# Attention with an MLP in float32 pieces: forms of the early units, g written over h, and new due times

## Chip, cores and metric

The kernel runs on one core of a Trainium2 chip. The metric is the device time of one execution in microseconds; three runs of the kernel before gave a median of 235.07 us (234.83 to 237.4).

## What is computed

A linear attention with a quadratic feature map, 4 batches, 4 heads, 1088 positions, head size 32, and behind it an MLP on 4352 tokens of 128 features with 2048 hidden units. All in float32; the inputs arrive as float64 words for the weights and for S, which the kernel turns into float32 itself.

```python
def phi(x):
    a = np.einsum('rd,bhsd->bhsr', S1, x)
    b = np.einsum('rd,bhsd->bhsr', S2, x)
    return np.einsum('bhsi,bhsj->bhsij', a, b).reshape(*x.shape[:-1], r * r)
kv = np.einsum('bhsf,bhsd->bhfd', k_p, v)
num = np.einsum('bhsf,bhfd->bhsd', q_p, kv)
den = np.einsum('bhsf,bhf->bhs', q_p, z)[..., None] + 1e-06
h = x @ w_in
g = np.where(h >= 1, h, np.where(h <= -1, 0.0, (h + 1) ** 2 / 4))
out = g @ w_out
```

## The kernel before

**Attention.** For each batch b, `keys(b, ...)` projects the keys with S (tiles abk, then transposed to kab), forms the products kp, sums z over them and builds kv and its turned copy kvb. `queries(b, ...)` does the same for the queries (abq, cq for the denominator, den, ap, qp, the transposed qt) and gathers the result into nd, from which x_hi and x_lo are cut: x rounded to float32r, and the rest. Batch 0 is done in four groups of positions, numbered 0 to 3 (nd0_1 is the gather of group 1), batches 1 to 3 in one gather of four banks each (nd1 is that of batch 1).

**The MLP.** The tokens lie in 9 chunks of 512 (the last has 256). A unit u is one chunk with one block j of 128 hidden units; there are 144. The first two chunks are woven in runs of four units, and so are the last two; the others follow each other. `unit(u)` (line 799) does the following:

- TensorE: h, three passes of float32r (x_hi wi_hi, x_lo wi_hi, x_hi wi_lo; L807 to L809) into one PSUM bank.
- ScalarE: s from h (L822), and its square (L824).
- VectorE: the clamp of h and s to g (L827).
- In most units g is split into g_hi, rounded to float32r, and g_lo, the rest (L838). TensorE adds three passes to the chunk's accumulator acc (L848, L849, L852).
- In a direct unit the clamp alone is made, and TensorE multiplies g as it stands with the whole piece of w_out (o32) in float32, L855; such a product shows as two passes in the trace.

So a unit has one of four kinds, for which this document uses the letters of the change:

| kind | g lies in | g_hi by | g_lo by | down product |
|---|---|---|---|---|
| w | SBUF | none | none | one in float32 |
| v | SBUF | VectorE, a second clamp | GpSimd | three passes |
| c | SBUF | ScalarE, a cast (L834) | GpSimd | three passes |
| p | PSUM | ScalarE, a cast | VectorE | three passes |

Before, the kind follows from shares by stretch: FP (w), IN_PSUM (p) and HI_ACT (c). A p unit holds two banks, that of h and one more for g.

**The weights.** `weights` loads pieces of 512 columns (i0 to i3, o0 to o3) into three raw buffers; `from_double` (line 395) makes the float32 value in several steps on ScalarE, GpSimd and VectorE, with a bank m (mi, mo) in between, and cuts it into hi (ScalarE) and lo (GpSimd). Where units of a group of four blocks are w, the piece of w_out is kept whole in o32.

**The order.** The program is written out by a planner, class Plan (line 91). Each step has a due time, an engine, an estimated cost, what it reads and what it writes. The planner plays the engines forward, and each free engine takes the ready step that is due first and has its buffers. There are 8 PSUM banks in the ring ps. The resulting order is fixed: on the chip each engine takes its instructions one after the other and waits at a semaphore where an input is not there. Due times come from tables: FK, FKV and FQ (keys and queries of batch 0), KEYS, QEND and QLONG (the later batches, counted in units), LOADS (their loads), I0, I1, WI, O0, O1, WO and OW (the weights). KP_POOL and QP_POOL name the pieces of kp and qp that GpSimd makes; the others are VectorE's. Until 15.82 us of its own time the planner fills TensorE's pauses with products of ones, called warm.

```python
plan.add(u, "PE", 3 * rounded(n), up, r=[...], w=[h]).kind(0, 6)
g = bank(f"g{u}") if late else Buf("g_hi", f"gd{u}", [P, CH]) if direct else Buf("g", f"g{u}", [P, CH])
plan.add(u, "DVE", dve(n), lambda: clamp(g), r=[h, s], w=[g])
if tag == "o" and c in fp_units:
    keep = whole[c] = Buf("o32", f"o32_{c}", [P, WC])
```

## Time and profile before

| what | value |
|---|---|
| median of three runs | 235.07 us (234.83 to 237.4) |
| span of the profiled execution, first to last instruction | 233.1 us |
| TensorE (PE) busy | 225.6 us, 97% |
| VectorE (DVE) busy | 197.9 us, 85% |
| ScalarE (ACT) busy | 191.8 us, 82% |
| GpSimd (POOL) busy | 195.1 us, 84% |
| DMA, mean over the span | 59 GB/s |

The profiled execution is described by its span; what lies around it is the difference to the time of a run. Busy times are unions of an engine's instructions; instructions of one engine overlap by some 0.1 us, so from one start to the next it takes less than one lasts. PEld are the weight loads of TensorE, which lie beside its passes. In a timeline a bracket at the end of a row tells the idle time of the engine before it and what ended it, as inferred from semaphores.

### The profile page before, as it was taken

The page shows a single profiled execution, that of the slowest core. Times are in us where ns is not written, and L with a number is a line of the kernel's source. Part 1 is how long each engine was busy: PE and PEld are TensorE (multiplying, and loading weights), DVE is VectorE, ACT ScalarE, POOL GpSimd, SP SyncE. Part 2 cuts the span into 40 slices and gives each one's busy share as a digit, 9 for nine tenths or more (in the row PEclk, how much of TensorE's full clock was granted, in tenths as well). Part 3 has the DMA queues.
Part 4 walks back from the last instruction along what each step waited for, and adds up shares of the span by engine and source line. Part 5 has one row for each costly group of instructions (what it writes and reads, how often), then busy time and mean ns, then how long its engine had stood idle before and what let it go on. Part 6 is the DMA issues. An engine that isn't in the chain of part 4 may idle for free.

```text
span 233.1 us, 4932 instructions
## 1 busy us (share of the span) xinstructions
PE 225.6 (97%) x1741; PEld 171.1 (73%) x1743; DVE 197.9 (85%) x379; ACT 191.8 (82%) x388; POOL 195.1 (84%) x175
## 2 busy tenths in 40 slices
PE   7979999999999999999999999999999999999994
PEld 2646656767768867876788688888788888888893
DVE  2479999999776989998869999997999589679983
ACT  3257999999998997884799669997897899499994
POOL 5796608678676799999998999999979899969991
PEclk9999999999999999999999999999999999999999
DMA  6960770750001100001000010001000100010001
...
DMA packets 4775, 13.86 MB, mean 59 GB/s; under 512 B 528, under 2 KB 912, under 8 KB 4752
## 3 DMA queue, kind: packets, MB, share of 16 engines
...
q8 instruction: 13, 0.21, 0.4%
q14 instruction: 10, 0.08, 0.1%
...
## 4 chain that ended last, share of the span: by engine, by line
PE 90%; DMA 4%; DVE 2%; issue 1%; ACT 1%; POOL 0%; SPq 0%; POOLq 0%
PE h L807 13%; PE acc L852 13%; PE h L808 13%; PE h L809 13%; PE acc L848 12%; PE acc L849 12%; PE acc L855 5%; DMA q<-in_qT 2%; PE nd L748 2%; DMA k<-in_kT 2%; PE kv L564 2%; PE warm L334 1%; PE abq L611 1%; PE abk L505 1%; PE cq L617 1%
## 5 line engine op out<-in xcount | busy, mean ns | idle before, releaser
L838 POOL TENSOR_TENSOR g_lo<-g,g_hi 128x512 fp32r<-128x512 f32 (+1 forms) x121 | 146.9, 1246 | 14.3 <-DVE g_hi L827 9.0
L827 DVE SCALAR_TENSOR_TENSOR g<-h,s 128x512 f32<-128x512 f32 (+1 forms) x131 | 83.7, 649 | 18.6 <-ACT s L824 15.6
L822 ACT ACTIVATE s<-h 128x512 f32<-128x512 f32 (+1 forms) x144 | 79.6, 572 | 16.0 <-PE h L809 13.3
L824 ACT ACTIVATE s<-s 128x512 f32<-128x512 f32 (+1 forms) x144 | 85.1, 613 | 2.2
L827 DVE SCALAR_TENSOR_TENSOR g_hi<-h,s 128x512 fp32r<-128x512 f32 (+1 forms) x98 | 63.9, 656 | 1.7 <-POOL g_lo L838 0.9
L807 PE MATMUL h<-x_hi,wi_hi 128*128 128x512 f32 (+1 forms) x144 | 58.0, 403 | 0.1
L808 PE MATMUL h<-x_lo,wi_hi 128*128 128x512 f32 (+1 forms) x144 | 54.9, 381 | 0.0
L809 PE MATMUL h<-x_hi,wi_lo 128*128 128x512 f32 (+1 forms) x144 | 54.6, 379 | 0.0
L848 PE MATMUL acc<-g_hi,wo_hi 128*128 128x512 f32 (+1 forms) x131 | 50.6, 388 | 0.0
L849 PE MATMUL acc<-g_hi,wo_lo 128*128 128x512 f32 (+1 forms) x131 | 49.4, 377 | 0.0
L852 PE MATMUL acc<-g_lo,wo_hi 128*128 128x512 f32 (+1 forms) x131 | 46.6, 389 | 0.0
L807 PEld LDWEIGHTS h<-x_hi,wi_hi 128*128 128x128 f32 x144 | 27.1, 188 | 8.1 <-PE h L809 0.6
L808 PEld LDWEIGHTS h<-x_lo,wi_hi 128*128 128x128 f32 x144 | 27.1, 188 | 6.5 <-issue 1.7
L809 PEld LDWEIGHTS h<-x_hi,wi_lo 128*128 128x128 f32 x144 | 27.1, 188 | 5.3
L852 PEld LDWEIGHTS acc<-g_lo,wo_hi 128*128 128x128 f32 x131 | 24.3, 188 | 7.0 <-issue 2.1
L848 PEld LDWEIGHTS acc<-g_hi,wo_hi 128*128 128x128 f32 x131 | 24.6, 188 | 6.2 <-issue 1.4
L849 PEld LDWEIGHTS acc<-g_hi,wo_lo 128*128 128x128 f32 x131 | 24.6, 188 | 4.7 <-issue 0.5
L834 ACT CAST g_hi<-g 128x512 fp32r<-128x512 f32 (+1 forms) x33 | 18.2, 562 | 2.6 <-DVE g L827 2.4
L529 POOL TENSOR_TENSOR kp<-kab 128x768 f32<-128x768 f32 (+2 forms) x8 | 15.1, 1901 | 2.9 <-DVE kab L511 2.9
L649 POOL TENSOR_TENSOR qp<-ap,qab 128x768 f32<-128x768 f32 x8 | 12.0, 1516 | 1.5 <-DVE ap L644 1.5
L855 PE MATMUL acc<-gd,o 128*128 128x512 f32 x26 | 12.9, 592 | 0.0
L827 DVE SCALAR_TENSOR_TENSOR gd<-h,s 128x512 f32<-128x512 f32 x13 | 8.7, 679 | 0.8 <-ACT s L824 0.8
(100 smaller groups left out, 176.7 us busy)
## 6 DMA issues: line engine op xcount, KB each, us to landing
...
```

The source lines that it names most:

```text
L807: nc.tensor.matmul(t[:, :n], lhsT=wi_hi[:, fj], rhs=x_hi[:, xs], start=True, stop=False)
L808: nc.tensor.matmul(t[:, :n], lhsT=wi_hi[:, fj], rhs=x_lo[:, xs], start=False, stop=False)
L809: nc.tensor.matmul(t[:, :n], lhsT=wi_lo[:, fj], rhs=x_hi[:, xs], start=False, stop=True)
L822: plan.add(u, "ACT", act(n), lambda: nc.scalar.activation(of(s)[:, :n], of(h)[:, :n], AF.Relu, bias=0.5, scale=0.5), r=[h], w=[s])
L824: plan.add(u, "ACT", act(n, False), lambda: nc.scalar.activation(of(s)[:, :n], of(s)[:, :n], AF.Square), w=[s])
L827: nc.vector.scalar_tensor_tensor(out=of(out)[:, :n], in0=of(h)[:, :n], scalar=1.0, in1=of(s)[:, :n], op0=ALU.max, op1=ALU.min)
L834: plan.add(u, "ACT", act(n, False), lambda: nc.scalar.copy(of(g_hi)[:, :n], of(g)[:, :n]), r=[g], w=[g_hi])
L838: plan.add(u, "DVE" if late else "POOL", dve(n) if late else pool_t(n), lambda: eng.tensor_tensor(out=of(g_lo)[:, :n], in0=of(g)[:, :n], i ...
L848: nc.tensor.matmul(of(acc)[:, :n], lhsT=wo_hi[:, fj], rhs=of(g_hi)[:, :n], start=first, stop=False)
L849: nc.tensor.matmul(of(acc)[:, :n], lhsT=wo_lo[:, fj], rhs=of(g_hi)[:, :n], start=False, stop=False)
L852: nc.tensor.matmul(of(acc)[:, :n], lhsT=wo_hi[:, fj], rhs=of(g_lo)[:, :n], start=False, stop=last)
L855: nc.tensor.matmul(of(acc)[:, :n], lhsT=of(whole[j // JW])[:, j % JW * P : (j % JW + 1) * P], rhs=of(g)[:, :n], start=first, stop=last)
```

## The change

Four things change.

1. The kinds of units 0 to 47 are spelled out in a word, KINDS; later units are c by a share CAST = 0.23 and v otherwise; the last four are p as before. FP, IN_PSUM and HI_ACT are gone.
2. A p unit has no bank of its own for g: the clamp writes over h.
3. `from_double` may leave a weight piece's value in its bank m and split it there, for the pieces named in IN_BANK = ('o0',), unless the piece is kept whole.
4. Nearly all due times and both lists of GpSimd's pieces have new numbers. KP_POOL gains (1, 0), QP_POOL loses (3, 0) and (3, 2).

Counted from the two rules, units of each kind:

| units | before | after |
|---|---|---|
| 0 to 31 | w 13, v 9, c 6, p 4 | w 8, v 8, c 11, p 5 |
| 32 to 47 | v 11, c 3, p 2 | v 8, c 5, p 3 |
| 48 to 143 | v 78, c 14, p 4 | v 71, c 21, p 4 |

```diff
-FP = (0.86, 0.57, 0.27, 0)
-OW = (2.26, 14.08, 3.92, 10.35)
+KINDS = 'wwwcpwwcwvcwvpcvvwcpvccccpvvpccvvvvvcvvvccppcvcp'
+IN_BANK = ('o0',)
+CAST = 0.23
+OW = (1.48, 6.15, 3.08, -14.76)
...
-LOADS = {1: (-1.49, 7.13, -0.36), 2: (9.25, 9.39, 31.26), 3: (58.3, 55.18, 44.56)}
-HI_ACT = (0.86, 0.38, 0.22, 0.15)
+LOADS = {1: (-1.2, 3.71, -5.47), 2: (17.53, 13.45, 26.52), 3: (55.55, 68.14, 43.66)}
...
-        full = keep or mag
+        banked = not keep and tag in IN_BANK
+        full = mb if banked else keep or mag
...
-                out=of(full).bitcast(I32), in0=lw(), scalar=29, in1=m(),
+                out=m() if banked else of(full).bitcast(I32), in0=lw(), scalar=29, in1=m(),
...
-        plan.add(due, "ACT", act(n, False), lambda: nc.scalar.copy(hi, of(full)), r=[full], w=[toks[0]])
-        plan.add(due, "POOL", pool_t(n), lambda: nc.gpsimd.tensor_tensor(
-            out=lo, in0=of(full), in1=hi.bitcast(F32), op=ALU.subtract), r=[full, toks[0]], w=[toks[1]])
+        value = lambda: of(full)[:, :n]
+        plan.add(due, "ACT", act(n, banked), lambda: nc.scalar.copy(hi, value()), r=[full], w=[toks[0]])
+        eng = nc.vector if banked else nc.gpsimd
+        plan.add(due, "DVE" if banked else "POOL", dve(n) if banked else pool_t(n), lambda: eng.tensor_tensor(
+            out=lo, in0=value(), in1=hi.bitcast(F32), op=ALU.subtract), r=[full, toks[0]], w=[toks[1]])
...
+    def kind_of(u):
+        if u >= len(units) - LATE:
+            return "p"
+        if u < len(KINDS):
+            return KINDS[u]
+        return "c" if int((u + 1) * CAST) > int(u * CAST) else "v"
+
+    fp_units = {units[u][2] // JW for u in range(len(units)) if kind_of(u) == "w"}
...
-        late = u >= len(units) - LATE or int((u + 1) * IN_PSUM[part]) > int(u * IN_PSUM[part])
-        direct = u in fp_units.get(j // JW, ())
-        late = late and not direct
-        g = bank(f"g{u}") if late else Buf("g_hi", f"gd{u}", [P, CH]) if direct else Buf("g", f"g{u}", [P, CH])
+        kind = kind_of(u)
+        late, direct = kind == "p", kind == "w"
+        g = h if late else Buf("g_hi", f"gd{u}", [P, CH]) if direct else Buf("g", f"g{u}", [P, CH])
...
-            share = 1.0 if late else HI_ACT[part]
-            if int((u + 1) * share) > int(u * share):
+            if kind in "pc":
```

How the order of the instructions moves is shown at three places. First TensorE around the projection of batch 1's queries (abq1, cq1). Before, it stands behind unit 6 and the first down product:

```order
L809 MATMUL h6_577<-x_hi_93,wi_lo_90 128x512
L848 MATMUL acc0_586<-g_hi0_558,wo_hi_91 128x512
L849 MATMUL acc0_586<-g_hi0_558,wo_lo_92 128x512
L611 MATMUL abq1_0_594<-q1_521,s_pair_97 32x288 x4
L611 MATMUL abq1_1_599<-q1_521,s_pair_97 32x288 x4
L617 MATMUL cq1_608<-q1_521,back_z_100 32x288 x4
L852 MATMUL acc0_586<-g_lo0_581,wo_hi_91 128x512
L807 MATMUL h7_620<-x_hi_93,wi_hi_89 128x512
```

In the changed order the same projection, with q1 loaded earlier, stands ahead of unit 0 and of the last transpositions of batch 0 (tp0_3):

```order
L539 MATMUL z1_410<-kab1_379 32x32 x4
L614 MATMUL abq1_0_437<-q1_285,s_pair_97 32x288 x4
L614 MATMUL abq1_1_442<-q1_285,s_pair_97 32x288 x4
L707 MATMUL tp0_3_0_452<-ident_66,qp0_3_407 128x128 x2
L707 MATMUL tp0_3_1_456<-ident_66,qp0_3_407 128x128 x2
L814 MATMUL h0_463<-x_hi_93,wi_hi_89 128x512
L815 MATMUL h0_463<-x_lo_94,wi_hi_89 128x512
L816 MATMUL h0_463<-x_hi_93,wi_lo_90 128x512
L814 MATMUL h1_471<-x_hi_93,wi_hi_89 128x512
```

Units 0 to 3 moved ahead of the gather nd0_3 and of the sums kv1, which before stood in front of unit 0; cq1 comes after them, ahead of unit 4.

Second, TensorE ahead of batch 1's gather nd1. Before, it follows unit 29:

```order
L852 MATMUL acc0_586<-g_lo24_961,wo_hi_91 128x512
L807 MATMUL h29_997<-x_hi_93,wi_hi_89 128x512
L808 MATMUL h29_997<-x_lo_94,wi_hi_89 128x512
L809 MATMUL h29_997<-x_hi_93,wi_lo_90 128x512
L848 MATMUL acc0_586<-g_hi25_970,wo_hi_91 128x512
L849 MATMUL acc0_586<-g_hi25_970,wo_lo_92 128x512
L748 MATMUL nd1_0_1009<-qt1_707,kvb1_535 32x288
```

In the changed order it follows unit 23, with the down products of units 18 to 20 between; ahead of these rows stand h22 and the w product of unit 17:

```order
L814 MATMUL h23_910<-x_hi_93,wi_hi_89 128x512
L815 MATMUL h23_910<-x_lo_94,wi_hi_89 128x512
L816 MATMUL h23_910<-x_hi_93,wi_lo_90 128x512
L852 MATMUL acc0_586<-g_hi18_886,wo_hi_91 128x512
L853 MATMUL acc0_586<-g_hi18_886,wo_lo_92 128x512
L852 MATMUL acc512_659<-g_hi20_902,wo_hi_91 128x512
L853 MATMUL acc512_659<-g_hi20_902,wo_lo_92 128x512
L856 MATMUL acc0_586<-g_lo18_900,wo_hi_91 128x512
L856 MATMUL acc512_659<-g_lo20_914,wo_hi_91 128x512
L852 MATMUL acc0_586<-g_hi19_898,wo_hi_91 128x512
L853 MATMUL acc0_586<-g_hi19_898,wo_lo_92 128x512
L751 MATMUL nd1_0_939<-qt1_703,kvb1_645 32x288
```

The gather moved ahead by six units, and its four banks are those that units up to 22 leave.

Third, ScalarE in units 14 to 18, before:

```order
L822 ACTIVATE s14_773<-h14_754 128x512
L413 ACTIVATE mago3_776<-raw_o3_732 128x512
L824 ACTIVATE s14_773<-s14_773 128x512
L834 CAST g_hi13_789<-g13_778 128x512
L822 ACTIVATE s15_795<-h15_768 128x512
L822 ACTIVATE s16_800<-h16_785 128x512
L824 ACTIVATE s15_795<-s15_795 128x512
L824 ACTIVATE s16_800<-s16_800 128x512
L446 CAST wo_hi_91<-o32_2_781 128x512
L822 ACTIVATE s17_821<-h17_810 128x512
```

And with the change:

```order
L827 ACTIVATE s14_776<-h14_760 128x512
L414 ACTIVATE mago3_778<-raw_o3_705 128x512
L829 ACTIVATE s14_776<-s14_776 128x512
L838 CAST g_hi13_791<-h13_746 128x512
L827 ACTIVATE s15_798<-h15_770 128x512
L838 CAST g_hi14_805<-g14_794 128x512
L829 ACTIVATE s15_798<-s15_798 128x512
L827 ACTIVATE s16_820<-h16_786 128x512
L448 CAST wo_hi_91<-o32_2_809 128x512
L829 ACTIVATE s16_820<-s16_820 128x512
L827 ACTIVATE s17_837<-h17_815 128x512
```

Unit 14, w before, is c now and adds a cast; the cast of unit 13, p in both, reads g from h's bank.

## Rows read from the trace of the kernel before

**Rows 1.** The page: span, and busy time, share and instructions of each engine.
```profile
span 233.1 us, 4932 instructions
...
PE 225.6 (97%) x1741; PEld 171.1 (73%) x1743; DVE 197.9 (85%) x379; ACT 191.8 (82%) x388; POOL 195.1 (84%) x175
```

**Rows 2.** Windows: stretch and its length, then busy us (instructions) of each engine, clock.
```profile
30.00:70.00 40.00, 40.00 (x213) 27.14 (x206) 36.44 (x66) 38.54 (x73) 27.20 (x23) 1.00 0.29 110
70.00:100.00 30.00, 30.00 (x247) 23.07 (x246) 26.66 (x51) 26.41 (x52) 26.46 (x20) 1.00 0.05 19
...
100.00:230.00 130.00, 129.90 (x840) 104.90 (x838) 113.58 (x205) 108.89 (x218) 120.75 (x99) 1.00 0.03 11
```

**Rows 3.** Timeline of TensorE, 14 to 30 us: start, length, line, tiles, idle before.
```profile
14.45 0.38 PE L334 MATMUL warm<-const-bfloat16-1.0 128*128 128x512 bf16 x1
16.37 0.45 PE L722 MATMUL nd<-qt,kvb 64*32 64x128 f32 x16 [1.54 <-DVE den L682]
17.23 1.31 PE L704 MATMUL tp<-ident,qp 128*128 128x128 f32 x10
...
19.96 0.44 PE L704 MATMUL tp<-ident,qp 128*128 128x128 f32 x2
20.76 0.44 PE L704 MATMUL tp<-ident,qp 128*128 128x128 f32 x2 [0.36 <-DVE kp L529]
...
29.16 0.72 PE L611 MATMUL abq<-q,s_pair 64*32 64x288 f32 x16 [0.43 <-DMA q<-in_qT]
```

**Rows 4.** Chain of waits, 28 to 34 us: start, share of the chain, what.
```profile
30.93 0.23 PE h L807
...
31.63 0.86 PE acc L855 x2
```

**Rows 5.** Waits of SyncE's queue: us in total, times, longest.
```profile
SPq L390 <- DVE magi L430: 27.9, 3, 11.9
```

**Rows 6.** Timeline of VectorE, 14 to 22 us.
```profile
14.65 0.28 DVE L465 COPY kvb<-kv 128x128 f32<-128x128 f32 x1
...
17.67 0.84 DVE L511 STREAM_TRANSPOSE kab<-abk 128x288 f32<-128x288 f32 x2
18.43 0.67 DVE L422 TENSOR_SCALAR mi<-hci 128x512 int32<-128x512 int32 x1
19.02 0.29 DVE L465 CAST x_hi<-nd 128x128 fp32r<-128x128 f32 x1
19.23 1.48 DVE L529 TENSOR_TENSOR kp<-kab,abk 128x1280 f32<-128x1280 f32 x1
20.62 0.18 DVE L544 TENSOR_TENSOR zm<-z,blocks 128x32 f32<-128x32 f32 x1
20.72 1.01 DVE L734 TENSOR_TENSOR x_lo<-nd,x_hi 128x192 fp32r<-128x192 f32 x4
21.65 0.69 DVE L426 SCALAR_TENSOR_TENSOR mi<-raw_i,mi 128x512 int32<-128x512 int32 x1
```

**Rows 7.** Timeline of ScalarE at 14 us and from 25 us.
```profile
14.32 0.65 ACT L464 COPY qt<-tp 128x256 f32<-128x256 f32 x2 [0.25 <-PE tp L704]
...
25.34 0.60 ACT L822 ACTIVATE s<-h 128x512 f32<-128x512 f32 x1
25.82 0.63 ACT L446 CAST wo_hi<-o 128x512 fp32r<-128x512 f32 x1
26.33 0.65 ACT L824 ACTIVATE s<-s 128x512 f32<-128x512 f32 x1
26.87 1.09 ACT L822 ACTIVATE s<-h 128x512 f32<-128x512 f32 x2
```

**Rows 8.** Lines by form: count, busy us, mean ns of one, idle before.
```profile
L838 POOL TENSOR_TENSOR g_lo<-g,g_hi 128x512 fp32r<-128x512 f32 x109 | 138.6, 1301 | 14.3 <-DVE g_hi L827 9.0 <-ACT g_hi L834 2.3 <-PE acc L852 1.9
L827 DVE SCALAR_TENSOR_TENSOR g<-h,s 128x512 f32<-128x512 f32 x115 | 77.3, 681 | 18.0 <-ACT s L824 15.2 <-POOL g_lo L838 2.0
...
L426 DVE SCALAR_TENSOR_TENSOR mi<-raw_i,mi 128x512 int32<-128x512 int32 x4 | 2.8, 692 | 0.0
```

**Rows 9.** The page's DMA queues: packets, MB, share of 16 engines.
```profile
q8 instruction: 13, 0.21, 0.4%
```

More of the change, by code (lines that the diff above doesn't have):

```diff
@@ L31 @@
 QPR = 0.55
-FP = (0.86, 0.57, 0.27, 0)
-OW = (2.26, 14.08, 3.92, 10.35)
+KINDS = 'wwwcpwwcwvcwvpcvvwcpvccccpvvpccvvvvvcvvvccppcvcp'
+IN_BANK = ('o0',)
+CAST = 0.23
+OW = (1.48, 6.15, 3.08, -14.76)
 QB = 1
 TP = 0.109
-I0 = -12.99
+I0 = -15.17
 LATE = 4
-I1 = -1.34
-O1 = 3.81
-KP_POOL = ((0, 0), (0, 1), (0, 2), (1, 1), (2, 0), (2, 1), (3, 0), (3, 1))
-O0 = -0.52
-KEYS = {1: (-38.16, -35.97), 2: (-24.56, -18.73), 3: (-46, -38.32)}
-QEND = ((10.45, 11.77, 3.1), (7.08, 8.78, 10.15), (10.63, 8.96, 3.21))
-QLONG = (18.8, 14.34, 16.89)
-FQ = ((-7.77, 3.99), (-12.01, 2.79), (-5.76, 1.08), (-6.38, 7.82))
-FK = (-14.64, 7.16)
-FKV = 2.51
-WI = 4.97
-WO = 0.59
-IN_PSUM = (0.89, 0.08, 0.12, 0)
-QP_POOL = ((0, 0), (0, 2), (0, 3), (1, 0), (1, 1), (1, 2), (2, 0), (2, 2), (3, 0), (3, 1), (3, 2))
-KVM = 0.71
-LOADS = {1: (-1.49, 7.13, -0.36), 2: (9.25, 9.39, 31.26), 3: (58.3, 55.18, 44.56)}
-HI_ACT = (0.86, 0.38, 0.22, 0.15)
+I1 = -6.97
+O1 = 5.7
+KP_POOL = ((0, 0), (0, 1), (0, 2), (1, 0), (1, 1), (2, 0), (2, 1), (3, 0), (3, 1))
+O0 = -3.77
+KEYS = {1: (-37.63, -23.84), 2: (-23.98, -18.53), 3: (-45.49, -38.83)}
+QEND = ((10.85, 11.07, 1.43), (7.53, 9.58, 10.4), (20.57, 28.66, 3.64))
+QLONG = (19.56, 11.13, 19.72)
+FQ = ((-8.26, -0.26), (-14.97, 3.0), (-6.04, -0.07), (-6.75, 8.35))
+FK = (-17.6, 15.91)
+FKV = 3.42
+WI = 1.74
+WO = 1.33
+QP_POOL = ((0, 0), (0, 2), (0, 3), (1, 0), (1, 1), (1, 2), (2, 0), (2, 2), (3, 1))
+KVM = 0.07
+LOADS = {1: (-1.2, 3.71, -5.47), 2: (17.53, 13.45, 26.52), 3: (55.55, 68.14, 43.66)}
 def word_as_float(bits):
@@ L789, in tile_kernel @@
         first_of.setdefault(c0, u)
-    fp_units = {}
     whole = {}
-    for u in range(2 * NJ):
-        part = u // 8
-        if int((u + 1) * FP[part]) > int(u * FP[part]):
-            fp_units.setdefault(part, set()).add(u)
+    def kind_of(u):
[5 more added lines that the diff above has]
+    fp_units = {units[u][2] // JW for u in range(len(units)) if kind_of(u) == "w"}
     accs = {}
@@ L813, in unit @@
         s = Buf("s", f"s{u}", [P, CH])
-        part = min(u // 16, 3)
-        late = u >= len(units) - LATE or int((u + 1) * IN_PSUM[part]) > int(u * IN_PSUM[part])
-        direct = u in fp_units.get(j // JW, ())
-        late = late and not direct
-        g = bank(f"g{u}") if late else Buf("g_hi", f"gd{u}", [P, CH]) if direct else Buf("g", f"g{u}", [P, CH])
+        kind = kind_of(u)
+        late, direct = kind == "p", kind == "w"
+        g = h if late else Buf("g_hi", f"gd{u}", [P, CH]) if direct else Buf("g", f"g{u}", [P, CH])
         if not direct:
```

## Prediction

> **What bounds the kernel now.** I read the page's busy shares first, then the busy time by stretch, then TensorE's own timeline, and only then the engines that feed it. The shares put four engines between 82% and 97% [rows 1], which says little by itself. The stretches say more: from 30 to 70, 70 to 100 and 100 to 230 us TensorE is busy 40.00 of 40, 30.00 of 30 and 129.90 of 130 us, at a granted clock of 1.00, the 2.4 GHz level [rows 2]. So from about 21 us on there is no gap in TensorE's work, and no other engine ends a wait there. The reader is to see in the timeline that all idle time left on TensorE after its warm-up lies in three gaps before 30 us: 1.54 us before the gather nd of batch 0, 0.36 us before a transposition, 0.43 us before the projection of batch 1's queries [rows 3]. Work saved on VectorE, ScalarE or GpSimd therefore gives nothing by itself. Time can come from three places alone: less work for TensorE, those gaps, and, on the wrong side, new gaps in the stretches that have none.
>
> The profiled execution spans 233.1 us [rows 1]. The three timed runs have a median of 235.07 us, so 2.0 us lie around the span; nothing in the change touches them, and I add every term to 235.07.
>
> **Part 1: five units fewer with the whole-precision product.** Kind w costs TensorE 0.86 us for its one down product, read from its two passes; any other kind costs three passes, and three passes of h run from 30.93 to 31.63, 0.70 us [rows 4]. 13 units are w before, 8 after: 5 x (0.86 - 0.70) = 0.8 us less work on an engine that never waits. **Term: -0.8 us.** It lies wholly on the path.
>
> **Part 2: the front.** The gap of 0.36 us ends on VectorE's kp [rows 3]. There VectorE makes a piece of kp for batch 1, from 19.23 to 20.72 with its successors behind [rows 6]. KP_POOL now holds (1, 0), so GpSimd makes this piece and the gap's cause goes. The gap of 0.43 us ends on the DMA of q1 [rows 3]. That load stands behind raw_i2 in SyncE's queue, and SyncE waited there for VectorE's magi, 11.9 us at the longest [rows 5]. In the changed queue q1 stands ahead of raw_i2, so it no longer waits for that buffer, and the projection is moved ahead of unit 0. Nothing else has to be late for these two to go: **-0.79 us.**
>
> What comes late next? In the new order TensorE does, after the gathers that ended at 19.96, the projection (0.72), two transpositions (0.44), units 0 to 3 (4 x 0.70) and one small z product, and then comes nd0_3 at about 24.0 [rows 3, 4]. Its bank is that of mo0, which VectorE releases with o32_0. VectorE starts its transpositions at 17.67 and has before that release: two transpositions 0.76, an mi step 0.59, a cast 0.21, then mi and magi 2 x 0.6, four x_lo 0.93, mo0 and the two steps that follow 3 x 0.6, two more transpositions 0.76 and zm 0.1, together 6.35 us, so 24.0 [rows 6]. Equal to within 0.1 us: **+0.1 us**, between 0 and 0.5 if VectorE starts that list late. The 1.54 us before the first gather I leave as it is. Its named releaser is den of VectorE, but the order shows kvb0 and two copies as its inputs, and the copy to kvb had started at 14.65 and took 0.28 [rows 6]; the gather could have begun near 15. I take it for new code of TensorE, whose queue q8 moved 13 packets in all, 16 KB each [rows 9]; no row dates them. The number of TensorE's rows ahead of this gather is unchanged.
>
> The Trainium skill, "Runtime: NRT & Kernel Launch", section "Instruction fetch mechanics", has code refilled in blocks of 16 KB and the crossing "mostly hidden". The size agrees with q8's 13 packets, but if my reading of this gap is right, 1.54 us were not hidden. By the rule the gap would belong to VectorE, and since ScalarE loses one copy ahead of den's input it would shrink by that copy, 0.3 us by the pair in [rows 7]: 233.7 in place of the sum below.
>
> **Part 3: who feeds TensorE.** The bare work of one unit, read from start to start: ScalarE 0.48 for s, 0.54 for its square and 0.51 for a cast [rows 7], VectorE 0.68 at most for a clamp, GpSimd 1.30 at most for g_lo [rows 8]; TensorE needs 1.4. Kinds c and p add a cast on ScalarE. In units 0 to 31 there are 10 casts before and 16 after: 6 x 0.51 = 3.1 us more. In units 0 to 47 it is 15 and 24: 4.6 us more. VectorE's passes in units 0 to 31 are the same 45 (one each, one more for v and p). GpSimd gets 4 more g_lo there, 5.2 us, and was idle 12.8 us from 30 to 70 [rows 2]. So the engine to watch is ScalarE: from 30 to 70 us it was idle 40 - 38.54 = 1.5 us, from 70 to 100 us 3.6 us [rows 2]. It falls behind TensorE by about 3.1 - 1.5 = 1.6 us by unit 31 and gets that back later. A unit's h stays in its bank that much longer. The place where this bites is batch 1's gather nd1, which needs four banks at once and now stands behind h23, not h29. Its last bank is that of h22, free when g22 is made: s 0.48, a weight cast that the new order puts between 0.51, square 0.54, clamp 0.68, with two handovers of 0.05 (kp ends at 20.71 and its reader starts at 20.76 [rows 3, 6]) 2.3 us after h22. TensorE has in that time a w product 0.86, h23 0.70 and eight passes of 0.23, 3.4 us [rows 4, 7, 8]. The slack is 1.1 us, against a lag of at most 1.6: between 0 and 0.5 us here. For this and like places in units 8 to 47 I take **+0.4 us**; the ends are 0, if the idle time of 70 to 100 us suffices, and 4.6, if none of it can be used.
>
> **Part 4: g over h.** A p unit clamps into the bank it reads. VectorE already does that in before, mi over mi, at 692 ns against 681 for the clamp into other memory [rows 8]: 12 x 0.01 us on an engine that isn't the bound, so 0. Ten banks that held g fall away. That could let h start earlier, but in a stretch where TensorE has no gap there is nothing to win; where ScalarE lags, it is what keeps the 0.4 us from being more. The split of a weight piece from its bank does nothing here: IN_BANK names o0, but weights() gives that piece a kept copy since units of group 0 are w, and then banked is false. Its wo_lo stays on GpSimd in the order. After unit 48 the change is 7 casts in place of 7 clamps, ScalarE +3.6 us over 130 us in which TensorE waited 0.1 us [rows 2]; 0. The last units keep their kinds and the end of the chain its order; 0.
>
> Sum: -0.8 - 0.79 + 0.1 + 0.4 = -1.1, **234.0 us**. Its own range, from the bounds above: 233.5 if no wait is new, 235.4 if the new waits make 1.9 us.
>
> **Rivals.** *A: ScalarE becomes the bound of units 8 to 47.* From the casts alone it has 4.6 us more to do there. For it: in 30 to 70 us it is 96% busy already [rows 2], each pause of it is a wait for h or g that comes again, and no work is taken from it but a few copies. Against it: the lag may be carried into the stretch after 70 us, where 3.6 us are idle. It decides from the point at which the lag passes the slack of 1.1 us at nd1 and goes on growing; if all 4.6 us come back as gaps on TensorE, the time is 235.07 - 1.5 + 4.6 = 238.2 us, and with half of it 235.9. *B: the work moved only moves the gaps.* The front's list on VectorE is even with TensorE's to within 0.1 us, and the seven waits on it from tp0_3 to nd0_3 have little room; if they cost what part 2 saves, only the 0.8 us and the 0.4 us of part 3 stay, 234.7, and with another 0.4 us nothing, 235.1. *C: the big gap goes as well.* If the 1.54 us depend on how the loads lie around 14 us, where k1 and v1 have changed places, they could vanish: 234.0 - 1.5 = 232.5 us. Against it: as many bytes are queued ahead of it as before, and q1 comes right behind.
>
> **How the numbers follow.** A measurement of this kernel tells about 1% (2.4 us) from no change. Forecast 0.58, B 0.14, A 0.18, C 0.10. Forecast and B lie within 1% altogether. Of A, 0.14 is above 237.4 and 0.04 below it. All of C is under 232.7. That gives faster 0.10, same 0.76 and slower 0.14. The range runs from 232.7 to 236.9: it leaves out most of C and the upper part of A.
>
> **What would show it.** Right: the waits of TensorE name no DMA of q and no kp before 30 us; the down product L859 has 16 passes, two for each of 8 units; TensorE is idle under 1 us in all from 21 us to its end, and that idle time ends on VectorE's g or on nd's banks; the gap before the first gather is again 1.3 to 1.8 us. Wrong: TensorE's busy time under 39 of 40 us in some stretch from 30 to 100 us with ScalarE over 98% busy (A), gaps at h0, z or nd0_3 that sum to over 0.7 us (B), or a gap under 0.5 us at the first gather (C). If the time is slower with TensorE still gapless, then its passes have become slower, and I have no row for that.

## The result, and the profile after

The changed kernel takes 232.3 us (median of 4 runs, 231.86 to 232.59), the kernel before 235.91 us in the 4 runs beside it; the ratio is 0.9861, with a 95% interval of 0.9827 to 0.9896. In five later sets of 19 to 31 runs the kernel before had medians from 234.99 to 235.47 us, so the change is worth about 2.7 to 3.6 us. The forecast was 234.0 us, 1.1 us less than before; the time lies 0.4 us under 232.7, the low end of the range.

The page of the changed kernel, which answers to [rows 1], and its instruction queue, to [rows 9]:

```profile
span 230.1 us, 4927 instructions
...
PE 223.8 (97%) x1746; PEld 171.7 (75%) x1748; DVE 194.8 (85%) x377; ACT 195.2 (85%) x397; POOL 198.3 (86%) x177
...
q8 instruction: 14, 0.23, 0.4%
```

TensorE is busy 1.8 us less than before and ScalarE 3.4 us more. The stretches, which answer to [rows 2] (stretch and its length, then busy us of PE, PEld, DVE, ACT and POOL, then clock):

```profile
30.00:70.00 40.00, 40.00 (x222) 29.91 (x221) 37.28 (x67) 39.17 (x78) 33.71 (x29) 1.00 0.24 87
70.00:100.00 30.00, 30.00 (x247) 22.88 (x246) 27.72 (x50) 27.47 (x55) 26.81 (x20) 1.00 0.05 19
```

ScalarE is now busy 39.17 of 40 us, 0.63 us more than before, and TensorE still has no gap. The waits of TensorE (releaser: us in total, times, longest):

```profile
PE nd L725 <- DVE den L687: 1.5, 1, 1.5
PE warm L334 <- PEq L963: 0.8, 1, 0.8
PE z L539 <- issue: 0.3, 1, 0.3
PE warm L334 <- issue: 0.2, 1, 0.2
```

The waits on q1 and on kp are gone, and none has come in their place. TensorE's timeline answers to [rows 3]:

```profile
14.04 0.38 PE L334 MATMUL warm<-const-bfloat16-1.0 128*128 128x512 bf16 x1
15.96 0.45 PE L725 MATMUL nd<-qt,kvb 64*32 64x128 f32 x16 [1.53 <-DVE den L687]
...
18.76 0.56 PE L725 MATMUL nd<-qt,kvb 64*32 64x192 f32 x16
19.25 0.27 PE L539 MATMUL z<-kab 128*32 128x32 f32 x8
19.45 0.72 PE L614 MATMUL abq<-q,s_pair 64*32 64x288 f32 x16
...
20.69 0.47 PE L814 MATMUL h<-x_hi,wi_hi 128*128 128x512 f32 x1
...
23.55 0.40 PE L816 MATMUL h<-x_hi,wi_lo 128*128 128x512 f32 x1
23.88 0.44 PE L725 MATMUL nd<-qt,kvb 64*32 64x128 f32 x16
```

The gap before the first gather is 1.53 us, as before 1.54. The projection abq1 runs at 19.45, unit 0 begins at 20.69, and nd0_3 comes at 23.88 without a gap. One product of a direct unit in the chain of waits (start, share of the chain), which answers to [rows 4]:

```profile
44.48 0.86 PE acc L859 x2
```

And all of them in the groups by line and form (busy us, mean ns of one):

```profile
L859 PE MATMUL acc<-gd,o 128*128 128x512 f32 x16 | 8.2, 592 | 0.0
```

16 passes, two for each of 8 units.

**A measure that repeats.** All that differs lies between the first pass of the first gather and TensorE's last passes. I call this the stretch: from the gather's start to the start of the last pass but one, 15.96 to 226.29, 210.3 us; in before 213.2 us. What lies ahead of it varies by execution (the gather starts between 14.65 and 16.67 us in the runs below). The stretch of one order repeats where no wait on a transfer lies in it: e9, whose four compute engines have the order of the changed kernel, has 210.34 against 210.33. The kernel before has 213.2 and, in e18, 214.1; 0.8 us of this difference is a longer wait on q1. In e10 and e11 part of a projection stands ahead of the gather, so their stretch holds less work than the others. The table gives the stretch with the number of blocks, which are counted from TensorE's timeline: a block is a run of small products (abk, abq, cq, z, kv, nd, tp) between passes of 128x512, the one that begins with the first gather included.

| run | median us | ratio, 95% interval | stretch us | blocks |
|---|---|---|---|---|
| before | 235.0 to 235.9 | | 213.2 | 16 |
| changed | 232.3 | 0.9861, 0.9827 to 0.9896 | 210.3 | 16 |
| e1 old forms | 236.48 | 1.0043, 1.0013 to 1.0072 | 214.8 | 19 |
| e2 old due times | 237.07 | 1.0077, 1.0055 to 1.0099 | 215.4 | 16 |
| e3 own bank | 233.56 | 0.9935, 0.9908 to 0.9962 | 211.9 | 19 |
| e4 fewer warm | 234.64 | 1.0009, 0.9971 to 1.0046 | 214.1 | 21 |
| e5 kp on VectorE | 234.75 | 0.9988, 0.9963 to 1.0014 | 212.9 | 16 |
| e6 q1 late | 242.17 | 1.031, 1.028 to 1.034 | 219.1 | 22 |
| e7 g over h alone | 236.29 | 1.007, 1.005 to 1.0091 | 215.8 | 19 |
| e8 13 more w | 235.92 | 1.0025, 0.9993 to 1.0057 | 214.3 | 19 |
| e9 k1 first | 232.48 | 0.9848, 0.9763 to 0.9934 | 210.3 | 16 |
| e10 2 warm less | 235.24 | 0.998, 0.9939 to 1.0021 | 212.3 | 20 |
| e11 4 warm less | 234.66 | 0.9998, 0.9953 to 1.0043 | 214.0 | 20 |
| e12 o3 in its bank | 233.68 | 0.9911, 0.988 to 0.9942 | 211.9 | 19 |
| e13 q1 in place | 234.84 | 0.9991, 0.9964 to 1.0018 | 213.0 | 16 |
| e14 kp in place | 236.6 | 1.0056, 1.0029 to 1.0083 | 215.0 | 16 |
| e15 g over h in place | 234.74 | 0.9988, 0.9953 to 1.0024 | 214.4 | 16 |
| e16 all three in place | 236.04 | 1.0049, 1.0018 to 1.008 | 213.9 | 16 |
| e17 kv1 later too | 235.71 | 1.0009, 0.9978 to 1.004 | 214.1 | 17 |
| e18 before again | 235.29 | 1.0017, 0.9991 to 1.0043 | 214.1 | 16 |

### The profile page after: what moved, and what is told of

The parts are those of the page before. It is cut to its first block, busy times and chain, and to the rows that moved or that the text cites. A ratio compares the mean times of both kernels' runs of the same rounds, so it can differ in the third digit from the quotient of the medians.

```text
span 230.1 us, 4927 instructions
## 1 busy us (share of the span) xinstructions
PE 223.8 (97%) x1746; PEld 171.7 (75%) x1748; DVE 194.8 (85%) x377; ACT 195.2 (85%) x397; POOL 198.3 (86%) x177
## 4 chain that ended last, share of the span: by engine, by line
PE 96%; POOL 1%; ACT 1%; issue 1%; DVE 0%; ACTq 0%
PE h L814 14%; PE h L815 14%; PE h L816 14%; PE acc L856 13%; PE acc L852 13%; PE acc L853 13%; PE acc L859 3%; PE warm L334 3%; PE nd L751 2%; PE kv L567 2%; PE abk L508 1%; PE abq L614 1%; PE tp L707 1%; PE z L539 1%; PE nd L725 1%; PE cq L620 1%
## 5 line engine op out<-in xcount | busy, mean ns | idle before, releaser
L842 POOL TENSOR_TENSOR g_lo<-g,g_hi 128x512 fp32r<-128x512 f32 (+1 forms) x124 | 150.7, 1252 | 17.1 <-DVE g_hi L832 7.6
L832 DVE SCALAR_TENSOR_TENSOR g<-h,s 128x512 f32<-128x512 f32 (+1 forms) x124 | 79.9, 655 | 17.6 <-ACT s L829 16.9
L832 DVE SCALAR_TENSOR_TENSOR g_hi<-h,s 128x512 fp32r<-128x512 f32 (+1 forms) x87 | 56.8, 654 | 2.3 <-POOL g_lo L842 0.6
L816 PE MATMUL h<-x_hi,wi_lo 128*128 128x512 f32 (+1 forms) x144 | 54.6, 379 | 0.0
L853 PE MATMUL acc<-g_hi,wo_lo 128*128 128x512 f32 (+1 forms) x136 | 51.2, 378 | 0.0
L856 PE MATMUL acc<-g_lo,wo_hi 128*128 128x512 f32 (+1 forms) x136 | 48.9, 393 | 0.0
L838 ACT CAST g_hi<-g 128x512 fp32r<-128x512 f32 (+1 forms) x37 | 22.3, 608 | 3.7 <-PE acc L853 2.0
L532 POOL TENSOR_TENSOR kp<-kab 128x768 f32<-128x768 f32 (+2 forms) x9 | 17.6, 1966 | 2.5 <-DVE kab L514 2.5
L652 POOL TENSOR_TENSOR qp<-ap,qab 128x768 f32<-128x768 f32 x6 | 9.1, 1517 | 0.7 <-DVE ap L647 0.7
L334 PE MATMUL warm<-const-bfloat16-1.0 128*128 128x512 bf16 x23 | 8.0, 475 | 1.0 <-PEq L963 0.8
L657 DVE STREAM_TRANSPOSE qt<-qp 128x768 f32<-128x768 f32 x9 | 8.7, 969 | 0.0
```

The source lines that it names most:

```text
L532: eng.tensor_tensor(out=of(kp)[:, grp[0] : grp[-1] + 1].rearrange("p t (h i j) -> p (t h) i j", h=H, i=R), in0=x[0].unsqueeze(3).broadcast ...
L816: nc.tensor.matmul(t[:, :n], lhsT=wi_lo[:, fj], rhs=x_hi[:, xs], start=False, stop=True)
L832: nc.vector.scalar_tensor_tensor(out=of(out)[:, :n], in0=of(h)[:, :n], scalar=1.0, in1=of(s)[:, :n], op0=ALU.max, op1=ALU.min)
L838: plan.add(u, "ACT", act(n, False), lambda: nc.scalar.copy(of(g_hi)[:, :n], of(g)[:, :n]), r=[g], w=[g_hi])
L842: plan.add(u, "DVE" if late else "POOL", dve(n) if late else pool_t(n), lambda: eng.tensor_tensor(out=of(g_lo)[:, :n], in0=of(g)[:, :n], i ...
L853: nc.tensor.matmul(of(acc)[:, :n], lhsT=wo_lo[:, fj], rhs=of(g_hi)[:, :n], start=False, stop=False)
```

## Experiments

### Forms and due times apart

e1 is the changed kernel with the kinds that the old shares gave, spelled as a word; e2 has the new kinds and code with the old due times and lists of pieces.

```diff
-KINDS = 'wwwcpwwcwvcwvpcvvwcpvccccpvvpccvvvvvcvvvccppcvcp'
+KINDS = 'vwwwwwwpwcwpwpwwvvwvvcwcpvcvcvvcvpvvcvvvcpvvvcvvvvvvvcvvvvvcvvvvvvcvvvvvvcvvvvvcvvvvvvcvvvvvvcvvvvvcvvvvvvcvvvvvvcvvvvvcvvvvvvcvvvvvvcvvvvvcpppp'
```

> The changed kernel with the old kinds spelled out as a word of 144 letters (w 13, v 98, c 23, p 10; p still writes g over h); due times and lists as changed. Theory F (the front: q1 and kp in time, fewer waits of TensorE before 30 us, and fewer changes between small and full passes, is what the prediction mis-sized; forms give only 5 x 0.17 us): ratio to before 0.990, some 0.9 us above the changed kernel. Theory S (the forms matter: ScalarE's casts and banks take hidden waits off TensorE between 30 and 110 us, and this is what was not foreseen): ratio 0.994 or above, 1.5 us or more above the changed kernel, with starts of full passes more than 0.27 us apart between 30 and 110 us that no w product explains.

```diff
-KP_POOL = ((0, 0), (0, 1), (0, 2), (1, 0), (1, 1), (2, 0), (2, 1), (3, 0), (3, 1))
+KP_POOL = ((0, 0), (0, 1), (0, 2), (1, 1), (2, 0), (2, 1), (3, 0), (3, 1))
...
-LOADS = {1: (-1.2, 3.71, -5.47), 2: (17.53, 13.45, 26.52), 3: (55.55, 68.14, 43.66)}
+LOADS = {1: (-1.49, 7.13, -0.36), 2: (9.25, 9.39, 31.26), 3: (58.3, 55.18, 44.56)}
```

> The changed kernel's code and kinds (w 8, v 87, c 37, p 12, g over h) with all due times and both lists of pieces as before. Theory F: only the 0.85 us of the w products come, ratio 0.996, and the waits on q1 (0.43 us) and kp (0.36 us) are there again. Theory S: ratio 0.992 or below, since the forms carry at least half of the 3.2 us.

Both halves alone are slower than the kernel before, 1.0043 and 1.0077, and together they give 0.9861. So neither theory held for both runs: forms and due times are no two gains that add up. Only S's sign in e1 came: full passes up to 0.57 us apart, at 42.3 us, that no w product explains. Of the waits of TensorE in e2:

```profile
PE acc L853 <- POOL wo_lo L450: 1.3, 1, 1.3
PE abq L614 <- DMA q<-in_qT: 0.9, 1, 0.9
...
PE tp L707 <- DVE kp L532: 0.4, 1, 0.4
```

The two waits of the front are there again, and a weight piece comes 1.3 us too late: GpSimd makes the third wo_lo from 55.06 us on, in the kernel before from 49.23.

### One entry taken back

In e3 a p unit has its own bank for g, as before.

```diff
-        g = h if late else Buf("g_hi", f"gd{u}", [P, CH]) if direct else Buf("g", f"g{u}", [P, CH])
+        g = bank(f"g{u}") if late else Buf("g_hi", f"gd{u}", [P, CH]) if direct else Buf("g", f"g{u}", [P, CH])
```

> The changed kernel with a bank of its own for g in p units again, all else as changed. Theory F: within 0.3% of the changed kernel (ratio to before 0.985 to 0.989), since TensorE is not short of banks. Theory S: at least 0.7 us slower than the changed kernel (ratio 0.989 or above), with waits of h on VectorE's g or g_lo of p units in units 4 to 47.

The loss is 0.7% against the changed kernel, the size that S said, and 1.5 us in the stretch; but most of it isn't a wait for the bank. The planner writes another order, with 19 blocks in place of 16. The chain of waits shows the blocks; each of its pieces runs from the end of one pass or product to the end of the next. In the changed kernel abq, kv and cq of one time are one block:

```profile
111.26 0.23 PE acc L856
111.50 0.65 PE abq L614 x16
112.14 0.58 PE kv L567 x32
112.72 0.48 PE cq L620 x8
113.21 0.43 PE acc L852
113.64 0.24 PE acc L853
```

In e3, the same kinds of products with full passes between them:

```profile
109.11 0.65 PE abq L614 x16
...
109.95 0.43 PE acc L852
...
112.92 0.70 PE kv L567 x40
113.61 0.49 PE cq L620 x8
...
114.55 0.43 PE acc L856
```

From start to start, a full pass among its like takes 0.23 us and a small product 0.02. At the edges of a block it is more: the last pass ahead of it takes 0.23 to 0.33, its last product 0.03 to 0.34, and the first pass behind it 0.31 to 0.34. What the edges take beyond the usual lengths sums to 4.9 us in the changed kernel and 6.0 in e3: 1.2 us for three blocks, some 0.4 each. The rest of the loss lies in two spacings of full passes, 0.40 at 51.85 and 0.44 at 120.45. At the first of them the weight load of h waits for VectorE's g, the kind of wait that S named (0.3 us with the pass behind it):

```profile
52.25 0.19 PEld L814 LDWEIGHTS h<-x_hi,wi_hi 128*128 128x128 f32 x1 [0.44 <-DVE g L832]
```

The busy shares don't show any of this, nor do the waits of TensorE's passes, which are those of the changed kernel line by line. Whether the changed order without g over h would lose anything wasn't tried.

e5 takes the piece (1, 0) of kp back to VectorE (the line of KP_POOL shown for e2, alone), e6 gives q1's load the due time 12.0, e12 puts o3 in place of o0 into IN_BANK. e8 makes 13 units between 48 and 111 w.

> The changed kernel with (1, 0) taken out of KP_POOL, so that VectorE makes this piece of kp for batch 1 again; all else as changed. Theory T (terms add): each part of the change is worth its own term, and the kp wait in the front is worth about 0.6 us from start to start of TensorE's passes, so taking it back gives 232.9 us, a ratio of 0.988, with a gap of 0.3 to 0.5 us before a transposition or a unit ahead of 30 us. Theory J (joint fit): kinds, banks and due times are one order, and any entry taken back costs more than its own term, since the planner then sends other instructions ahead: a ratio of 0.993 or more, and the loss is not at kp but spread over 20 to 100 us.

```diff
-LOADS = {1: (-1.2, 3.71, -5.47), 2: (17.53, 13.45, 26.52), 3: (55.55, 68.14, 43.66)}
+LOADS = {1: (-1.2, 12.0, -5.47), 2: (17.53, 13.45, 26.52), 3: (55.55, 68.14, 43.66)}
```

> The changed kernel with the due time of q1's load at 12.0, so that q1 stands behind one more weight piece in SyncE's queue, as before the change; all else as changed. T: the wait on q1 comes back, 0.4 to 0.5 us, 232.8 us, ratio 0.988, with a gap before abq1 that names DMA q. J: 0.993 or more.

```diff
-IN_BANK = ('o0',)
+IN_BANK = ('o3',)
```

> The changed kernel with IN_BANK = ('o3',) in place of ('o0',): o3 is the one piece of w_out that is not kept whole, so its value is now made in the bank mo3 and split there, wo_lo by VectorE in place of GpSimd. T: GpSimd's step of 1.3 us goes, VectorE's of 0.6 comes, on engines that TensorE doesn't wait for: 0.985 to 0.989. J: the planner's order moves from about unit 16 on: 0.993 or more, with small spacings over 0.35 us between TensorE's passes after 45 us.

```diff
-KINDS = 'wwwcpwwcwvcwvpcvvwcpvccccpvvpccvvvvvcvvvccppcvcp'
+KINDS = 'wwwcpwwcwvcwvpcvvwcpvccccpvvpccvvvvvcvvvccppcvcpwwwwcvvvcvvvcvvvwcwwvcvvvcvvvvcvwwcwvvcvvvvcvvvcwwwcvvvvcvvvcvvv'
```

> The changed kernel with 13 units between 48 and 111 (v before, blocks 0 to 3 of their chunks) made w: a price for the whole-precision product where TensorE has no gap. The product is the same computation. T: 13 x (0.86 - 0.70) = 2.1 us more work on TensorE, 234.4 us, ratio 0.995, with TensorE still gapless. J or anything where TensorE isn't the bound: below 0.989 (nothing lost, since VectorE and GpSimd lose 13 passes each) or above 1.000.

T's sums failed in e5, e6 and e8, where J's bounds were met; e12, at 0.9911, lies between T's 0.989 and J's 0.993, and its interval holds both. e5 loses 2.5 us of stretch with the same 16 blocks, 2.2 of them ahead of 86 us in small stalls (its waits name magi, mago and gd of VectorE, 0.2 to 0.3 us each). e12 loses 1.6 us: the edges of three blocks more take 1.2 of it, and at 60.41 us a unit's h starts 0.4 us late behind VectorE's wo_lo, for which its weight load waits and which is the edit's own step. e8 loses 3.9: thirteen products cost 13 x 0.17 = 2.2 us (0.86 from start to start against three passes of 0.23). So w has the price of the forecast, and the other 1.7 us are of the new order, with three blocks more and full passes 0.38 to 0.51 apart at 54.6, 59.0 and 127.6 us. e6 is another case (stretch and its length, busy us of the engines, clock):

```profile
28.00:30.00 2.00, 0.00 (x0) 0.00 (x0) 1.29 (x3) 2.00 (x5) 0.85 (x1) 1.00 1.02 406
...
32.00:34.00 2.00, 2.00 (x7) 0.86 (x4) 2.00 (x5) 0.00 (x0) 0.00 (x0) 0.50 0.04 13
```

TensorE waited 2.2 us for q1, and behind this wait its granted clock fell to 0.50, the 1.2 GHz level; a w product there lasts 2.08 us, against 1.02 at 34.92 us. What else makes up the 8.8 us of stretch that e6 loses wasn't taken apart.

e7 is the kernel before with g written over h in p units, re-planned:

```diff
-        g = bank(f"g{u}") if late else Buf("g_hi", f"gd{u}", [P, CH]) if direct else Buf("g", f"g{u}", [P, CH])
+        g = h if late else Buf("g_hi", f"gd{u}", [P, CH]) if direct else Buf("g", f"g{u}", [P, CH])
```

> The kernel before with one edit: a p unit writes g over h and has no bank of its own; kinds and due times as before. T: nothing, 0.997 to 1.003, since TensorE showed no gap from 30 us on. Theory B (banks by themselves): the ten banks that fall away let h start earlier; TensorE loses small stalls that its overlapping passes hide, and the ratio is 0.994 or below, as the own-bank run of the changed kernel lost 0.7%. J: the old due times were fitted to the old banks, 1.000 to 1.008.

It is slower, 1.007: 19 blocks again, and q1's wait is 1.3 us. B fell, and J's bound was met.

### The gap before the first gather

e4 stops the warm passes at 5 us of the planner's time (23 passes become 10). e9 puts k1's load ahead of v1's again; e10 and e11 do that with 2 and 4 passes fewer in TensorE's program.

```diff
-WARM = 15.82
+WARM = 5.0
```

> WARM = 5 in place of 15.82: 10 warm passes in place of 25, so TensorE has 30 rows (a weight load and a pass each) fewer behind it at the first gather of batch 0. Theory C (the 1.5 us gap is new code: it comes at TensorE's 449th row whatever that is): the gap is no longer in front of the first gather but some 30 rows later, inside the projection abk of batch 1 that follows, and is shorter, 0.5 to 1.3 us; the time falls by 0.3 to 1.0 us unless the clock falls. Theory D (the gap is a wait for VectorE, den or ap, as its row names it): it stays in front of the gather with 1.3 us or more. The granted clock tells whether fewer warm passes cost anything: under 0.99 in the first 20 us would.

```diff
-LOADS = {1: (-1.2, 3.71, -5.47), 2: (17.53, 13.45, 26.52), 3: (55.55, 68.14, 43.66)}
+LOADS = {1: (-1.2, 3.71, -1.0), 2: (17.53, 13.45, 26.52), 3: (55.55, 68.14, 43.66)}
```

> The changed kernel with k1's load ahead of v1's in SyncE's queue, as before the change; the order of the four other engines stays word for word. T: nothing waited for k1 in the changed kernel, so 0.985 to 0.988 and again 1.4 to 1.6 us before the first gather. J: an entry of the due times taken back, 0.993 or more, with a wait on v1 at the sums kv1.

e10 has WARM = 12.0 and e11 WARM = 10.0 beside this line.

> As e9, and two warm passes fewer ahead of the first gather, so that the gather stands four of TensorE's instructions (two passes and two weight loads) sooner. Theory V (the gap ahead of the first gather is a wait on VectorE's den or kvb): the gap of 1.3 to 1.7 us again ends at the gather's first pass. Theory K (new code for TensorE, which comes at a fixed place of its program): the gather starts 0.3 us or more after kvb is done and the gap stands behind its second pass, inside the gather. Time by either 0.983 to 0.988, as the warm passes fill a stretch in which TensorE waits anyway; if the granted clock falls to 0.5 ahead of 16 us, 0.990 or more.

> As e9, with about five warm passes fewer. K: the whole gather runs at once after kvb's copy, from about 15.0 us, and the gap falls behind it, at the projection abk1 or later; the time gains what the gather no longer waits, 0.3 to 0.8 us, 0.981 to 0.985. V: the gap stays ahead of the gather, 0.985 to 0.988. If the granted clock falls ahead of 14 us as in the run with 10 warm passes: above 0.990.

In e10 and e11 the planner sends abk1 ahead of the gather, and the gap stands inside abk1. TensorE's timeline of e10:

```profile
14.42 0.43 PE L508 MATMUL abk<-k,s_pair 64*32 64x288 f32 x1
16.18 0.47 PE L508 MATMUL abk<-k,s_pair 64*32 64x288 f32 x8 [1.33 <-issue]
```

And of e11:

```profile
14.28 0.68 PE L508 MATMUL abk<-k,s_pair 64*32 64x288 f32 x5
16.21 0.72 PE L508 MATMUL abk<-k,s_pair 64*32 64x288 f32 x6 [1.26 <-issue]
```

All passes of abk1 have the same inputs, k1 and s_pair, and some of them had run: in the middle of one projection TensorE waits for nothing that the profile shows, and in e11, with two warm passes fewer than in e10, the place is four passes later in abk1. Counted from the start of the program it is one place. From there to the end of the gap, in the changed kernel, in e10 and in e11 (stretch and its length, then busy us and instructions of the engines, clock):

```profile
0.00:15.90 15.90, 13.02 (x218) 7.01 (x220) 8.52 (x32) 6.33 (x16) 11.64 (x26) 1.00 0.87 333
0.00:16.10 16.10, 12.95 (x217) 7.01 (x220) 8.10 (x30) 6.49 (x17) 11.46 (x26) 1.00 0.87 330
0.00:16.15 16.15, 13.20 (x219) 6.87 (x220) 8.28 (x31) 6.51 (x17) 11.63 (x26) 1.00 0.88 331
```

These are 438, 437 and 439 passes and weight loads. So the gap belongs to a place of TensorE's program, not to VectorE's den; new code, K, is the reading that fits. The planner of both kernels counts with it (HELD, BLOCK = 449, 256 in class Plan). The traces also date the packets of the instruction queue, which the prediction had no row for: the first 16 KB packet of q8 is on its way from 14.05 to 15.01 us in the kernel before, from 13.53 to 14.47 in the changed one, 13.96 to 14.92 in e10 and 13.97 to 14.91 in e11, and TensorE goes on 1.3 to 1.5 us after it has come. What fills these 1.3 us is open. This is the reading that the prediction set against the Trainium skill's "mostly hidden" in "Runtime: NRT & Kernel Launch", "Instruction fetch mechanics": here 1.3 us (e11) to 2.1 us (e14) are not hidden, at one of the 14 such packets of the changed kernel; at the other 13 TensorE has no gap. The gap is ended at 16.2 to 16.6 us in e9 to e11, with more or fewer warm passes, so nothing was won. e10 and e11 lost stretch at other places (1.1 us before a unit's h and four more blocks in each). e4 started the gather at 14.65, but its granted clock was 0.50 from 10 to 12 us, abk1 then waited 1.0 us for k1, and its order has 21 blocks:

```profile
10.00:12.00 2.00, 2.00 (x58) 2.00 (x52) 1.97 (x9) 1.12 (x4) 2.00 (x2) 0.50 1.04 425
```

e9 is as fast as the changed kernel, as T said. No run beat it by more than can be told.

### One edit each in the old order

These runs leave the planner's order of the kernel before as it is, instruction by instruction, and move one thing in the list that it returns.

```diff
     order = plan.run()
+    at = {b.name: i for i, s in enumerate(order) if s.ways[0][0] == "SP" for b in s.ways[0][4]}
+    order.insert(at["raw_i2"], order.pop(at["q1"]))
```

> The kernel before with q1's load ahead of raw_i2 in SyncE's queue and nothing else: the order of the four other engines stays as it was, instruction by instruction. Theory G (a wait is worth the gap that the trace shows): TensorE's stretch from the first gather to its last pass, 213.2 us, shrinks by 0.43. Theory S (a wait is worth the excess from start to start, since an ended pass still lies over the next one's start): by 0.5. Theory M (the gain only moves): by less than 0.2, since the next instruction waits then. The ratio, 0.998 in all, tells little; the stretch is read from the trace.

```diff
-            def products(eng=eng, grp=grp, n=n, pool=pool):
+            swap = (b, gi) == (1, 0)
+            def products(eng=nc.gpsimd if swap else eng, grp=grp, n=n, pool=pool or swap):
```

> The kernel before with the one piece (1, 0) of kp emitted on GpSimd at the place where it stood, and nothing else. G: 0.36 us less in the same stretch, S: 0.5 us less, M: less than 0.2, or more time if GpSimd's g_lo come late behind it.

```diff
+        def at(b):
+            return of(h if late and b is g else b)
...
-            nc.vector.scalar_tensor_tensor(out=of(out)[:, :n], in0=of(h)[:, :n], scalar=1.0, in1=of(s)[:, :n],
+            nc.vector.scalar_tensor_tensor(out=at(out)[:, :n], in0=of(h)[:, :n], scalar=1.0, in1=of(s)[:, :n],
```

> The kernel before with g written over h in its ten p units, in the old order: the planner still counts a bank for g, the chip's ring of banks doesn't give one out. G and my forecast: nothing, within 0.1 us in the stretch. Theory B (free banks let h start earlier): 0.3 us less or more than that, and the spacing of 0.60 at 111.5 us, 0.39 at 68.8 us or the long w product at 44.4 us goes.

e16 has the three edits together (e15 and e16 also read g from h in the cast and in the step of g_lo).

> The three edits together in the old order. If waits add up: 0.8 us less by G, 1.0 us or more by S; the ratio 0.995 to 0.997. If the gain is of the new order as a whole (J), 0.998 to 1.002. What then is left to the changed kernel's 210.3 us is the five w units, 0.9 us, and what only the new due times give.

```diff
+    names = lambda s: [b.name for b in s.ways[s.taken][4]]
+    late = [s for s in order if "kv1" in names(s)]
+    order = [s for s in order if s not in late]
+    for unit_h, steps in (("h5", late[3:]), ("h3", late[:3])):
+        i = next(i for i, s in enumerate(order) if unit_h in names(s))
+        order[i + 1 : i + 1] = steps
```

> The kernel before with q1's load ahead of raw_i2, the piece (1, 0) of kp on GpSimd, and, in the old order otherwise, the sums kv1 with their copies moved behind units 3 and 5, as the changed order has them. Theory P (the piece on GpSimd is free only where kv1 stands later: in the old order kv1 waited twice 0.75 us for it): the two gaps before kv1 go, and TensorE's stretch from the first gather to its last pass is 212.2 us, 1.0 less than before, ratio 0.994 to 0.998. Theory M (each removed wait comes back elsewhere): a new gap of 0.5 us or more at h0 (x_lo comes late) or at abq1, and the stretch is 212.8 or more.

e18 is the kernel before itself.

> The kernel before, unchanged, for one more profiled execution. Theory Q (the wait on q1 differs from execution to execution, since its load runs beside raw_i2, k2 and q2 on the same DMA engines; the trace that the forecast read had the shortest one): a gap of 0.5 to 1.6 us before abq1 instead of 0.43, and the stretch from the first gather to the end 213.3 to 214.5 us. If the gap is again 0.40 to 0.46 and the stretch 213.2, the longer waits of the other runs are their edits'. Ratio 0.998 to 1.002 by either.

The place of the wait on q1 in TensorE's timeline of e13:

```profile
28.03 0.40 PE L849 MATMUL acc<-g_hi,wo_lo 128*128 128x512 f32 x1
28.35 0.71 PE L611 MATMUL abq<-q,s_pair 64*32 64x288 f32 x16
```

The same place in e18:

```profile
28.29 0.39 PE L849 MATMUL acc<-g_hi,wo_lo 128*128 128x512 f32 x1
29.92 0.68 PE L611 MATMUL abq<-q,s_pair 64*32 64x288 f32 x11 [1.24 <-DMA q<-in_qT]
```

From start to start it is 0.32 in e13, without the wait, and 1.63 in e18, with it, so the wait cost 1.3 us in this second execution of the kernel before; by the same reckoning 0.5 in the first, whose row shows 0.43 [rows 3]. Q held: the wait changes from execution to execution of one order (e15, whose queue has the same order, shows 1.6). In e13 it is gone at its place, as S said, but the stretch is only 0.23 shorter than in the first execution, since a stall near 68 us grew from 0.16 to 0.40 us. There an h waits for VectorE's x_lo, which did not come as much earlier as TensorE did:

```profile
68.61 0.47 PE L807 MATMUL h<-x_hi,wi_hi 128*128 128x512 f32 x1 [0.23 <-DVE x_lo L761]
```

In e15 the stretch is 1.17 longer than in the first execution, and q1's wait 1.16 longer: g over h is worth nothing here, as forecast. The piece of kp, in e14:

```profile
20.55 0.31 PE L551 MATMUL z<-zm,back 128*128 128x32 f32 x2
21.61 0.77 PE L566 MATMUL kv<-kp,v 128*32 128x64 f32 x40 [0.75 <-POOL kp L531]
...
23.53 0.65 PE L566 MATMUL kv<-kp,v 128*32 128x64 f32 x32 [0.78 <-POOL kp L531]
```

The wait of 0.36 us on VectorE is gone, and the sums kv1 wait twice for GpSimd in its place; abq1 then waits 0.9 us for a bank that VectorE's gd gives back. e16 adds the three edits: 213.9, 0.6 longer than the first execution. From start to start the two gaps of kv1 add 1.7 us, and kp's wait takes 0.6 and q1's 0.5 away. With kv1 moved behind units 3 and 5 (e17) these two gaps go and unit 0 starts 5.2 us after the first gather, not 6.6; then a product for q1's denominator waits for a bank:

```profile
29.02 0.72 PE L613 MATMUL abq<-q,s_pair 64*32 64x288 f32 x16
30.59 0.69 PE L619 MATMUL cq<-q,back_z 128*32 128x288 f32 x8 [0.85 <-DVE gd L829]
```

and the stretch is 214.1. M held, P fell: in the old order these edits together don't shorten the stretch. The new wait ends on VectorE's gd, which gives back the bank of a w unit.

## Why the prediction was wrong

The direction was right, and so were the price of w and the two waits that went; the sum was too small, and no single term makes up the difference. The stretch fell by 2.9 us. From start to start of TensorE's passes the two traces differ in these places:

| term | forecast | between the traces |
|---|---|---|
| five w units fewer | -0.8 | -0.86 (5 x 0.17) |
| wait on kp | -0.36 | -0.48 |
| wait on q1 | -0.43 | -0.51 (in e18's execution -1.3) |
| gather nd0_2 | 0 | -0.31 |
| stalls at 68.8 and 111.5 us | 0 | -0.58 |
| small new stalls at 99.0, 99.8 and 172.8 us | 0 | +0.23 |
| the rest: edges of blocks, changes between small products | 0 | -0.40 |
| new waits of parts 2 and 3 | +0.5 | 0 |
| sum | -1.1 | -2.91 |

**The step that failed is the reading that all idle time left on TensorE lies in three gaps before 30 us, and that "in a stretch where TensorE has no gap there is nothing to win".** A pass lasts 0.39 us in the trace, and the next one starts 0.23 after it; up to 0.16 us of waiting behind a pass shows no gap and counts as busy. Lost time that shows no gap, or only in part, makes up 1.3 us of the 1.8 that the sum was short of: 0.20 in the price of the two waits, 0.31 at nd0_2, 0.35 in stalls, 0.40 in the rest. The other 0.5 are the new waits, which did not come.

**Part 1** held: 16 passes, 0.86 a product, and e8 gave the same price.

**Part 2** took the price of the two waits from the gaps shown: 0.36 and 0.43 stood for some 0.5 each. And q1's wait was taken from one execution, which had the shortest of those of its order, 0.43 against 1.24 and 1.60 (e18, e15). How long it is in the median run isn't shown. "Nothing else has to be late for these two to go" was wrong of the edits (e14, e13) and right of the changed order, which moves kv1 behind unit 3 and abq1 ahead of unit 0. nd0_2 took 0.80 from start to start in the old order (e13, 18.85 to 19.65) and takes 0.49 now, 18.76 to 19.25. That it waited on a copy of qt is argued, not shown. The +0.1 at nd0_3 did not come: 0.33 from start to start at 23.55, a change of kind without a wait.

**Part 4's** "nothing to win" overlooked two stalls of the kernel before, which count as busy. TensorE's rows there, in which a full pass starts 0.39 and 0.60 us ahead of the next:

```profile
68.80 0.40 PE L849 MATMUL acc<-g_hi,wo_lo 128*128 128x512 f32 x1
69.18 0.47 PE L807 MATMUL h<-x_hi,wi_hi 128*128 128x512 f32 x1
...
111.46 0.51 PE L852 MATMUL acc<-g_lo,wo_hi 128*128 128x512 f32 x1
112.06 0.47 PE L807 MATMUL h<-x_hi,wi_hi 128*128 128x512 f32 x1
```

And VectorE's, behind the gathers nd1 and nd2:

```profile
68.59 1.15 DVE L761 TENSOR_TENSOR x_lo<-nd,x_hi 128x288 fp32r<-128x288 f32 x3
...
111.47 0.81 DVE L761 TENSOR_TENSOR x_lo<-nd,x_hi 128x288 fp32r<-128x288 f32 x2
```

Both times h starts 0.59 us after x_lo has begun, and in e13 0.60 after it (68.01 to 68.61), where the row names x_lo as the releaser. So TensorE waited there for the first piece of x_lo. In the changed kernel nd1 and nd2 stand elsewhere, and no full pass behind them is late; its own spacings over the usual are small, 0.28 and 0.30 at 99.0 and 99.8 us and 0.34 at 172.8. Which due time moved the gathers isn't shown. On g over h by itself part 4 was right where it could be tried: it gives nothing in the old order (e15).

**Part 3's +0.4 did not come.** ScalarE did get its work (39.17 of 40 us busy), and nd1 came without a wait. Rival A fell with it. **The gap before the first gather** stayed, and for the reason given (e10, e11); rival C fell. **Rival B** is what happens in the old order (e14, e16, e17), not in the changed one.

What the forecast had no term for is the order as a whole: three more blocks cost 1.2 us (e3, e12), and a re-planned order has them or not. The changed kernel has 16, like before, so most of this term is 0; that it would be was not argued. The sums above say where the time went. The runs don't divide the gain among the entries of the tables, so which of them it needs stays open.
